# A hand-written order for every engine up to the last weight conversion, with two token blocks sharing layer 1's first pass

## The chip, the cores and the metric

One core of a Trainium2 chip runs the whole program. Its engines are named as the profile names them: PE multiplies matrices (PEld loads its weights), DVE and ACT work on vectors, POOL does little here, and SP and ACT issue DMAs. The metric is the device time of one execution in microseconds (us); the median of three runs before the change is 971.0 us (968.24 to 971.59).

## What is computed

A linear attention with decay over 4 batches, 8 heads, 768 positions and a head size of 48, and behind it two feed-forward layers on 3072 tokens of 384 features with 2048 hidden features each:

```python
for t in range(S):
    state = alpha[:, :, t, :, None] * state + np.einsum('bhd,bhe->bhde', k[:, :, t], v[:, :, t])
    y[:, :, t] = np.einsum('bhd,bhde->bhe', q[:, :, t], state)
...
h = x @ w_in;  g = np.maximum(0.01 * h, h);                   x = g @ w_out     # layer 1
h = x @ w_in;  g = np.where(h > 0, h, np.exp(min(h, 0)) - 1);  x = g @ w_out    # layer 2
```

The weights arrive as 64-bit floats and are converted on the chip.

## The kernel before

**Attention** goes in 24 units of 128 positions (6 units make one batch; the state passes from a unit to the next within it). A unit's chain: `attn_prep` on DVE (a scan E from behind, pe, kS = k times E, a reciprocal, a scan F, qh = q times F); `attn_S` on PE (the scores `sc`, and a transpose `pk` of kS); `attn_S_post` (the mask A on DVE, a copy `kn` of pk on ACT, T on DVE); `attn_V` on PE (`po`, the unit's output, and `pu`, the state's update); `attn_V_post` (xh on ACT and xl on DVE, a two-part split of po, and the state S on DVE). The PSUM pool `ps_a` has three buffers for sc, pk, po and pu together. Four units make a **block** of 512 tokens; behind its last unit `gather` moves rows of x with six DMAs on SP, and only then can the block's first matrix product start.

**Layer 1** goes block by block, 16 steps m each. A step is `ffn1_h` (9 matmuls into hp), `ffn1_g` (t on ACT, max on DVE, gh on ACT, gl on DVE), and `ffn1_y` (9 matmuls that add up in three PSUM tiles y over the 16 steps). h runs two steps ahead of y (`LA = 2`). **Layer 2** does the same with other functions on six blocks.

**The weights of step m** (`both`, m = 0 to 15) are loaded by `stage1` with five DMAs on SP into one of four buffers (x2t0 to x2t3) and converted by `convert_p` (two ACT instructions), `convert_a` (three on DVE, L234, L235 and L237, and the high half on ACT, L238) and `convert_b` (the low half on DVE, L241). Block 0's step m needs conversion m; the other blocks need none.

**What sets the order.** The kernel is traced in one order, and the Tile scheduler then places instructions by its own forecast of when their operands are ready; only the first instruction of convert_p and of convert_a is pinned to program order. So attention, conversions and steps are interleaved by the scheduler. The main program (L574 to L670) runs units 0 to 3 with conversions between them, then block 0's steps with the conversions and with the pieces of units 4 to 7 among them, then the other blocks.

Of the kernel before, what the change touches and what calls it, by code (L numbers as in the profile page):

```python
# [8 lines left out]
F32 = mybir.dt.float32  # L9
# [10 lines left out]
def attention_two_layers_kernel(  # L20
# [79 lines left out]
    vts = {}  # L100
# [21 lines left out]
    def attn_prep(u):  # L122
# [3 lines left out]
        F = at_p.tile([PR, EXT], F32, tag="F", name="F")  # L126
# [5 lines left out]
        nc.vector.tensor_tensor_scan(F[:, 0:EXT - 1], t[:, 0:EXT - 1], d1[:, 0:EXT - 1], 0.0, ALU.mult, ALU.add)  # L132
        e2 = E[:, 1:EXT].rearrange("p (g c) -> p g c", c=C + 1)
        nc.vector.tensor_mul(kS, kS, e2[:, :, 1:C + 1])
        nc.vector.tensor_mul(qh, qh, ext(F, 0)[:, :, 1:C + 1])
        st[u] = dict(kS=kS, qh=qh, pe=pe)

    def attn_S(u):
        c = u % NC
        d = st[u]  # L140
        kS, qh = d["kS"], d["qh"]
        A = at_p.tile([128, 2, NP, C], F32, tag="A", name="A")
# [5 lines left out]
        d["A"], d["sc"] = A, sc  # L148
        if c < NC - 1:
            pk = ps_a.tile([128, NP, PR], F32, tag="at", name="pk")  # L150
            for p in range(NP):
                nc.tensor.transpose(pk[:, p, :], kS[:, p, :], ident[:PR, :PR])
            d["pk"] = pk

    def attn_S_post(u):
        c = u % NC
        d = st[u]
        for j, sc in enumerate(d.pop("sc")):
            nc.vector.tensor_mul(d["A"][:, j], sc, causal.unsqueeze(1).to_broadcast([128, NP, C]))
        if c < NC - 1:  # L160
# [3 lines left out]
        if c > 0:  # L164
# [3 lines left out]

    def attn_V(u):
        c = u % NC  # L170
        d = st[u]
        vt = vts.pop(u)
# [13 lines left out]
        d["po"] = po  # L186
        if c < NC - 1:
# [9 lines left out]
    def attn_V_post(u, xh, xl, off):  # L197
        c = u % NC
        d = st.pop(u)
        po = d["po"]  # L200
        nc.scalar.copy(xh[0:PR, :, off:off + C], po)
        nc.vector.tensor_sub(xl[0:PR, :, off:off + C], po, xh[0:PR, :, off:off + C].bitcast(F32))
        if c < NC - 1:
            pu = d["pu"]
            Sn = at_p.tile([PR, NP, D], F32, tag="S", name="S")
            if c > 0:
                nc.vector.tensor_add(Sn, pu, d["T"])
            else:
                nc.vector.tensor_copy(Sn, pu)
            st["S"] = Sn  # L210

# [48 lines left out]
    def ffn1_g(j, m):  # L260
        n = xt[j][2]
# [493 lines left out]
```

## Time and profile before

| | |
|---|---|
| Median of 3 runs | 971.0 us (968.24 to 971.59) |
| The profiled execution | 971.32 us, of which the span is 969.6 us |
| PE busy | 929.8 us (96% of the span), 5234 matmuls |
| DVE busy | 529.4 us (55%) |
| ACT busy | 445.8 us (46%) |
| The chain that ended last | PE 79%, DVE 8%, DMA 8%, ACT 2% |
| Last matmul ends | about 960 us; then copies and the last output DMA |

The span is divided into 40 slices on the page; PE's digits run 4679 and then 9 to the end, DVE's are 6 to 9 in the first seven slices (up to about 170 us) and fall to 3 later. A matmul's end is modelled, so a busy PE need not be a PE at its peak: what matmuls cost is read from the distance between starts where they follow each other without a break.

### The profile page before, as it was taken

Reading aid. Unit: us, or ns where it says so; the run is one execution under the profiler, and the core shown is the slowest. Engines: PE = TensorE matmul, PEld = TensorE weight load, DVE = VectorE, ACT = ScalarE, POOL = GpSimd, SP = SyncE. Lnnn points to the kernel's source line nnn. Section 1 sums busy time; section 2 is a strip of 40 time slices with the busy share of each in tenths; the row PEclk is TensorE's granted clock in tenths of the full one; section 3 lists DMA queues with packets and bytes.
Section 4 is the critical chain, followed back from the end, with each engine's and each line's share of the span. In section 5 each row is a group of like instructions: output and inputs, shape, how many; then the busy total and the mean of one; then the engine's idle time right before and its main releaser. Section 6 shows DMA issues by size and latency. Waiting matters only on the chain.

```text
span 969.6 us, 13094 instructions
## 1 busy us (share of the span) xinstructions
PE 929.8 (96%) x5234; PEld 781.8 (81%) x5234; DVE 529.4 (55%) x876; ACT 445.8 (46%) x783; POOL 1.1 (0%) x8
## 2 busy tenths in 40 slices
PE   4679999999999999999999999999999999999996
PEld 3557667887888788788878889999999999999995
DVE  6788998534555557454469983433433333333332
ACT  1344545322322323233367795574664744744442
POOL 0000000000000000000000000000000000000000
PEclk9969999999999999999999999999999999999998
DMA  9655561102111221211234330020100200100001
GB/s 243 184 152 160 153 181 45 29 13 58 42 41 41 58 71 53 58 41 50 58 96 141 115 98 10 1 81 1 62 20 1 72 10 1 62 0 1 33 1 37
DMA packets 25093, 62.38 MB, mean 64 GB/s; under 512 B 3936, under 2 KB 7008, under 8 KB 25024
## 3 DMA queue, kind: packets, MB, share of 16 engines
q1 hardware_dynamic: 19184, 40.54, 15.1%
q10 hardware_dynamic: 5840, 20.92, 7.5%
q8 instruction: 43, 0.70, 0.3%
q14 instruction: 26, 0.21, 0.1%
HBM read 54.37 MB, written 4.72 MB: 61 GB/s over the span
## 4 chain that ended last, share of the span: by engine, by line
PE 79%; DVE 8%; DMA 8%; ACT 2%; issue 1%; SPq 1%; DVEq 0%; ACTq 0%
PE hp L310 20%; PE hp L256 16%; PE y L281 15%; PE o L341 10%; PE oa L341 10%; DMA x2t<-in_w_dram 3%; DMA pack<-in_seqs_dram 2%; PE po L178 2%; DMA stg<-in_w_dram 2%; PE sc L147 2%; PE po L184 2%; DMA x<-x 1%; DVE x2t L235 1%; DVE t L265 1%; DVE gl L81 1%
## 5 line engine op out<-in xcount | busy, mean ns | idle before, releaser
L256 PE MATMUL hp<-x,w 128*128 128x512 f32 x864 | 218.6, 395 | 4.1 <-DMA x<-x 2.7
L310 PE MATMUL hp<-x,w 128*128 128x512 f32 x864 | 215.4, 393 | 0.0
L81 DVE TENSOR_TENSOR gl<-t,gh 128x512 fp32r<-128x512 f32 x192 | 132.7, 691 | 126.3 <-ACT gh L78 122.4
L78 ACT CAST gh<-t 128x512 fp32r<-128x512 f32 x192 | 119.0, 620 | 174.1 <-PE y L281 63.9
L256 PEld LDWEIGHTS hp<-x,w 128*128 128x128 f32 x864 | 160.4, 188 | 41.2 <-issue 3.2
L310 PEld LDWEIGHTS hp<-x,w 128*128 128x128 f32 x864 | 160.7, 188 | 29.3
L281 PE MATMUL y<-gh,w 128*128 128x512 f32 x576 | 173.2, 397 | 1.6 <-ACT gh L78 1.6
L319 DVE SCALAR_TENSOR_TENSOR t<-t,hp 128x512 f32<-128x512 f32 x96 | 66.0, 687 | 148.8 <-ACT t L318 148.8
L281 PEld LDWEIGHTS y<-gh,w 128*128 128x128 f32 x576 | 105.5, 188 | 25.6 <-ACT gh L78 3.0
L265 DVE TENSOR_TENSOR t<-t,hp 128x512 f32<-128x512 f32 x96 | 65.4, 683 | 73.8 <-ACT t L264 73.7
L281 PE MATMUL y<-gl,w 128*128 128x512 f32 x288 | 105.3, 394 | 0.0
L317 ACT ACTIVATE t<-hp 128x512 f32<-128x512 f32 x96 | 57.1, 595 | 103.7 <-PE hp L310 103.6
L264 ACT ACTIVATE t<-hp 128x512 f32<-128x512 f32 x96 | 56.8, 594 | 99.2 <-PE hp L256 99.2
L341 PE MATMUL oa<-w,gh 128*128 128x384 f32 x384 | 96.7, 337 | 0.0
L341 PE MATMUL o<-w,gh 128*128 128x384 f32 x384 | 94.7, 337 | 0.2 <-ACT x2t L292 0.2
L341 PEld LDWEIGHTS o<-w,gh 128*128 128x128 f32 x384 | 70.5, 188 | 6.0 <-ACT x2t L292 0.5
L341 PEld LDWEIGHTS oa<-w,gh 128*128 128x128 f32 x384 | 70.2, 188 | 2.9
L281 PEld LDWEIGHTS y<-gl,w 128*128 128x128 f32 x288 | 53.5, 188 | 12.1 <-issue 0.7
L341 PE MATMUL oa<-w,gl 128*128 128x384 f32 x192 | 63.0, 337 | 0.0
L318 ACT ACTIVATE t<-t 128x512 f32<-128x512 f32 x96 | 60.8, 633 | 2.3
L341 PE MATMUL o<-w,gl 128*128 128x384 f32 x192 | 61.0, 336 | 0.0
L147 PEld LDWEIGHTS sc<-pack 48*128 48x128 f32 x384 | 32.0, 210 | 20.3 <-issue 9.3
(89 smaller groups left out, 761.5 us busy)
## 6 DMA issues: line engine op xcount, KB each, us to landing
pack<-in_seqs_dram ACTq DMA_DIRECT2D x21, 674.2 KB, 4.8
stg<-in_w_dram SPq DMA_DIRECT2D x28, 384.0 KB, 3.4
x2t<-in_w_dram SPq DMA_DIRECT2D x20, 384.0 KB, 4.3
vt<-in_vals_dram ACTq DMA_DIRECT2D x21, 288.0 KB, 3.0
span<-in_seqs_dram SPq DMA_DIRECT2D x24, 226.2 KB, 2.7
x2t<-in_w_dram SPq DMA_DIRECT2D x32, 144.0 KB, 3.6
out_dram<-osb SPq DMA_DIRECT2D x24, 192.0 KB, 2.1
x<-x SPq DMA_DIRECT2D x36, 64.0 KB, 4.4
```

The costliest lines, as they stand in the source:

```text
L78: nc.scalar.copy(dst, src)
L81: (lo_engine or nc.vector).tensor_sub(lo, src, dst.bitcast(F32))
L147: nc.tensor.matmul(sc[j][:, p], lhsT=kS[r, p, :], rhs=qh[r, p, :], start=True, stop=True)
L256: nc.tensor.matmul(hp, lhsT=a[:, kk, :], rhs=x[:, kk, :n], start=(i == 0), stop=(i == 3 * KD - 1))
L264: nc.scalar.activation(t, hp, ACTF.Copy, scale=0.01)
L265: nc.vector.tensor_max(t, t, hp)
L281: nc.tensor.matmul(ytiles[j][c], lhsT=a[:, c * 128:(c + 1) * 128], rhs=x, start=(m == 0 and i == 0), stop=(m == KF - 1 and i == 2),)
L310: nc.tensor.matmul(hp, lhsT=a[:, kk, :], rhs=x[:, kk, :], start=(i == 0), stop=(i == 3 * KD - 1))
L317: nc.scalar.activation(t, hp, ACTF.Relu, scale=-1.0)
L318: nc.scalar.activation(t, t, ACTF.Exp, scale=-1.0)
L319: nc.vector.scalar_tensor_tensor(out=t, in0=t, scalar=-1.0, in1=hp, op0=ALU.add, op1=ALU.max)
L341: nc.tensor.matmul(otiles[j][i], lhsT=a[:, i * 128:(i + 1) * 128], rhs=x, start=(m == 0 and n == 0), stop=(m == KF - 1 and n == 2),)
```

## The change

Every instruction up to the step at which the sixteenth conversion is done is chained to the one traced before it on its engine (`in_order`), so on each engine the order is that of the program text; what is traced later is left to the scheduler, and `behind` puts the fallback program behind it. The attention functions are split into their parts (L122 to L257 of the new file), and `quarter(u, i)` runs parts of unit u and of unit u + 1 in a fixed order. Block 0 and block 1 run steps 0 to 3 each, then block 0 its steps 4 to 15, then block 1; y is stored in x2t after the first four steps and added to on DVE at the end. Units 4 to 7 run inside steps 0 and 1, none during the fifteen steps after that (s = 2 to 16), in which the conversions go on at three in four steps; from step 17 on the later units are spread as before. Loads of units 1 and 2 stand ahead of the weights on SP, and from conversion 4 on two weight buffers (x2t2, x2t3) alternate, since x2t0 and x2t1 hold y.

```diff
-        load_v(0)
         load_unit(1)
+        load_v(0)
+        load_unit(2)
+        load_v(1)
         stage1(0)
-        load_v(1)
-        stage1(1)
-        load_unit(2)
         load_v(2)
-        stage1(2)
-        stage1(3)
+        for m in range(1, 4):
+            stage1(m)
...
+        def quarter(u, i, chain=True):
...
+            if i == 0:
+                attn_pu(u)
+                prep_k(u + 1)
+                attn_T(u)
+            elif i == 1:
+                attn_mask(u)
+                if chain:
+                    attn_pk(u + 1)
+                    attn_kn(u + 1)
+                attn_po(u)
+            elif i == 2:
+                prep_F(u + 1)
+                attn_state(u)
+                prep_q(u + 1)
+                if chain:
+                    attn_sc(u + 1)
+                attn_xh(u, xh, off)
+                next_load(u + 3)
+            else:
+                attn_xl(u, xh, xl, off)
+                st.pop(u)
+                if u == blocks[j][0] + blocks[j][1] - 1:
+                    gather(t, blocks[j][1] * C)
...
+        for u in range(UB):
+            for i in range(3):
+                quarter(u, i)
+            if u > 1:
+                conv1.a(u - 1)
+            quarter(u, 3)
+            if u > 1:
+                conv1.b(u - 1)
+            if u > 0:
+                conv1.p(u)
...
+        head, tail = range(FIRST), range(FIRST, KF)
+        seq = [(1, j, m) for ms in (head, tail) for j in range(2) for m in ms]
...
+            if s <= KF:
+                c = 4 if s == 0 else 1 + FIRST + s - 2 - (s - 2) // 4 if s > 1 and s % 4 != 1 else 0
+                ffn1_y(j, m)
+                pe_h(n)
+                ffn1_t(n[1], n[2])
+                conv1.a(c)
+                if s < 2:
+                    for p in quarters[7 * s:7 * s + 7]:
+                        quarter(*p, chain=p[0] + 1 < UB + blocks[1][1])
+                ffn1_max(n[1], n[2])
+                ffn1_gh(n[1], n[2])
+                conv1.b(c)
+                ffn1_gl(n[1], n[2])
+                if c:
+                    conv1.p(c + 1)
+                in_order()
+                continue
```

Three places show how instructions move. The rows of an order name an engine's instructions as the profile does, but for the scans E and F, which stand as SCALAR_TENSOR_TENSOR.

DVE at units 1 and 2, before:

```order
L128 SCALAR_TENSOR_TENSOR E<-pack,d_96 112x517
L130 TENSOR_SCALAR pe<-E 112x4
L134 TENSOR_TENSOR pack<-pack,E 112x512
L202 TENSOR_TENSOR x<-po,x 112x4x128
L131 RECIPROCAL d_97<-pe 112x4
L159 TENSOR_TENSOR A<-sc_252,causal 128x512
L132 SCALAR_TENSOR_TENSOR F<-pack,d_97 112x516
L135 TENSOR_TENSOR pack<-pack,F 112x512
L128 SCALAR_TENSOR_TENSOR E<-pack,d_96 112x517
L159 TENSOR_TENSOR A<-sc_253,causal 128x512
```

and now:

```order
L240 TENSOR_TENSOR x<-po,x 112x4x128
L127 SCALAR_TENSOR_TENSOR E<-pack,d_96 112x517
L129 TENSOR_SCALAR pe<-E 112x4
L130 RECIPROCAL d_97<-pe 112x4
L132 TENSOR_TENSOR pack<-pack,E 112x512
L187 TENSOR_TENSOR T<-S,pe 112x192
L180 TENSOR_TENSOR A<-sc_252,causal 128x512
L180 TENSOR_TENSOR A<-sc_253,causal 128x512
L139 SCALAR_TENSOR_TENSOR F<-pack,d_97 112x516
L248 TENSOR_TENSOR S<-pu,T 112x192
L144 TENSOR_TENSOR pack<-pack,F 112x512
L240 TENSOR_TENSOR x<-po,x 112x4x128
```

The scan E of unit 3 no longer stands between the two halves of unit 1's mask A; each unit's xl (written to x) is followed by the first half of the preparation of the unit after next, and every unit has the same sequence.

DVE at the conversions, before (conversions 7 and 8 among units 5 to 7):

```order
L237 ISA x2t_138<-x2t_134,x2t_138 128x1536
L131 RECIPROCAL d_97<-pe 112x4
L81 TENSOR_TENSOR gl<-t,gh 128x512
L128 SCALAR_TENSOR_TENSOR E<-pack,d_96 112x517
L202 TENSOR_TENSOR x<-po,x 112x4x128
L209 COPY S<-pu 112x192
L241 TENSOR_TENSOR w_7_117<-x2t_139,w_7_116 128x768
L132 SCALAR_TENSOR_TENSOR F<-pack,d_97 112x516
L130 TENSOR_SCALAR pe<-E 112x4
L134 TENSOR_TENSOR pack<-pack,E 112x512
L241 TENSOR_TENSOR w_8_119<-x2t_138,w_8_118 128x768
```

and now (conversions 4 and 5, steps s = 2 and 3):

```order
L275 TENSOR_SCALAR x2t_138<-x2t_136 128x768
L276 SCALAR_TENSOR_TENSOR x2t_138<-x2t_138 128x768
L278 ISA x2t_138<-x2t_136,x2t_138 128x1536
L308 TENSOR_TENSOR t<-t,hp 128x512
L282 TENSOR_TENSOR w_4_111<-x2t_138,w_4_110 128x768
L318 TENSOR_TENSOR gl<-t,gh 128x512
L275 TENSOR_SCALAR x2t_139<-x2t_137 128x768
L276 SCALAR_TENSOR_TENSOR x2t_139<-x2t_139 128x768
L278 ISA x2t_139<-x2t_137,x2t_139 128x1536
L308 TENSOR_TENSOR t<-t,hp 128x512
L282 TENSOR_TENSOR w_5_113<-x2t_139,w_5_112 128x768
L318 TENSOR_TENSOR gl<-t,gh 128x512
```

There is no attention among the conversions any more: a step with a conversion is six instructions on DVE in a fixed order, and a step without one is two.

SP at the start, before:

```order
L107 DMA pack<-in_seqs_dram 112x517
L109 DMA pack<-in_seqs_dram 112x512
L116 DMA vt<-in_vals_dram 128x576
L111 DMA pack<-in_seqs_dram 112x1541
L411 DMA x2t_134<-in_w_dram 48x768
L412 DMA x2t_134<-in_w_dram 16x768
L411 DMA x2t_134<-in_w_dram 48x768
L412 DMA x2t_134<-in_w_dram 16x768
L413 DMA x2t_134<-in_w_dram 128x768
```

and now:

```order
L107 DMA pack<-in_seqs_dram 112x517
L109 DMA pack<-in_seqs_dram 112x512
L111 DMA pack<-in_seqs_dram 112x1541
L116 DMA vt<-in_vals_dram 128x576
L111 DMA pack<-in_seqs_dram 112x1541
L116 DMA vt<-in_vals_dram 128x576
L473 DMA x2t_134<-in_w_dram 48x768
```

The pack of unit 2, which stood behind two steps' weights, is now third, ahead of all weights.

## Rows read from the trace of the kernel before

**Rows 1.** Busy time by engine in three stretches: length, PE, PEld, DVE, ACT, POOL, granted PE clock, DMA.
```profile
0.00:61.00 61.00, 34.59 (x278) 27.84 (x278) 46.24 (x78) 17.29 (x23) 1.08 (x8) 0.88 0.75 199
61.00:164.00 103.00, 99.64 (x644) 73.11 (x646) 94.61 (x148) 49.16 (x73) 0.00 (x0) 0.97 0.51 142
164.00:960.00 796.00, 794.96 (x4316) 680.48 (x4313) 387.55 (x649) 378.46 (x685) 0.00 (x0) 1.00 0.15 44
```

**Rows 2.** The same for PE's L256 (h) and then L281 (y) alone.
```profile
61.00:164.00 103.00, 38.63 (x138) 0.97 0.51 142
...
61.00:164.00 103.00, 34.74 (x126) 0.97 0.51 142
```

**Rows 3.** The chain of waits where PE never stops: start, length, what.
```profile
217.81 2.04 PE hp L256 x9
219.84 1.09 PE sc L147 x16
220.94 2.27 PE y L281 x9
```

**Rows 4.** PE's timeline, same stretch: a unit's two po groups at full speed.
```profile
229.25 1.09 PE L178 MATMUL po<-A,vt 128*64 128x128 f32 x16
230.27 1.08 PE L184 MATMUL po<-pack,T 48*48 48x128 f32 x16
```

**Rows 5.** PE's timeline, first units: the same groups early on.
```profile
26.83 1.94 PE L178 MATMUL po<-A,vt 128*48 128x128 f32 x14 [1.57 <-DVE A L159]
...
30.58 2.08 PE L147 MATMUL sc<-pack 48*128 48x128 f32 x16
35.48 0.98 PE L152 MATMUL pk<-ident,pack 112*128 112x112 f32 x4 [2.82 <-DVE x L202]
42.71 1.19 PE L147 MATMUL sc<-pack 48*128 48x128 f32 x16
```

**Rows 6.** Busy time by engine in a short stretch; columns as in Rows 1.
```profile
54.00:56.00 2.00, 2.00 (x18) 1.77 (x16) 2.00 (x4) 0.91 (x2) 0.00 (x0) 0.50 0.50 149
```

**Rows 7.** DVE's timeline: one preparation, one mask, one xl, one convert_a.
```profile
4.71 1.23 DVE L128 TENSOR_TENSOR_SCAN E<-pack,d 112x517 f32<-112x517 f32 x1 [2.64 <-DMA pack<-in_seqs_dram]
6.86 1.23 DVE L132 TENSOR_TENSOR_SCAN F<-pack,d 112x516 f32<-112x516 f32 x1
...
13.86 1.28 DVE L159 TENSOR_TENSOR A<-sc,causal 128x512 f32<-128x512 f32 x2
...
55.56 0.69 DVE L202 TENSOR_TENSOR x<-po,x 112x512 fp32r<-112x512 f32 x1
...
87.05 0.56 DVE L234 TENSOR_SCALAR x2t<-x2t 128x768 int32<-128x768 int32 x1
...
88.71 0.96 DVE L237 CUSTOM_DVE_ANT_0 x2t<-x2t,x2t 128x1536 uint16<-128x1536 uint16 x1
```

**Rows 8.** ACT's groups up to 250 us: count, busy us, mean ns, idle time before.
```profile
L78 ACT CAST gh<-t 128x512 fp32r<-128x512 f32 x34 | 21.1, 621 | 39.2 <-DVE t L265 20.7 <-PE y L281 18.4
...
L230 ACT ACTIVATE x2t<-x2t 128x768 int32<-128x768 uint16 x16 | 14.6, 913 | 40.5 <-DMA x2t<-in_w_dram 39.0 <-PE po L178 1.5
L238 ACT CAST w<-x2t 128x768 fp32r<-128x768 f32 x16 | 13.3, 830 | 13.9 <-DVE x2t L237 13.9
L201 ACT CAST x<-po 112x512 fp32r<-112x512 f32 x12 | 6.9, 582 | 3.3 <-PE po L184 3.3
```

**Rows 9.** What DVE waited for up to 110 us: us in total, times, longest.
```profile
DVE E L128 <- DMA pack<-in_seqs_dram: 12.6, 8, 2.7
```

**Rows 10.** PE's timeline: block 0's first h.
```profile
61.19 1.19 PE L256 MATMUL hp<-x,w 128*128 128x512 f32 x2 [1.88 <-DMA x<-x]
```

**Rows 11.** Line L413, the last of a step's five weight loads: us to landing.
```profile
DMA to landing us min/median/max: 3.3/4.3/5.8
```

**Rows 12.** Timelines of ACT and of SP's queue: one issue of a DMA each.
```profile
30.95 0.35 ACTq L116 DMA_DIRECT2D vt<-in_vals_dram  x1
...
73.26 0.42 SPq L413 DMA_DIRECT2D x2t<-in_w_dram  x1
```

More of the change, by code (lines that the diff above doesn't have):

```diff
@@ L163, in attn_S_post, with attn_mask, attn_T @@
             d["kn"] = kn
-        if c > 0:
+    def attn_mask(u):
+        d = st[u]
+        A = at_p.tile([128, 2, NP, C], F32, tag="A", name="A")
+        for j, sc in enumerate(d.pop("sc")):
+            nc.vector.tensor_mul(A[:, j], sc, causal.unsqueeze(1).to_broadcast([128, NP, C]))
+        d["A"] = A
+    def attn_T(u):
+        d = st[u]
+        if u % NC > 0:
             T = at_p.tile([PR, NP, D], F32, tag="cT", name="T")
@@ L186, in attn_V, with attn_pu @@
         d["po"] = po
+    def attn_pu(u):
+        c = u % NC
+        d = st[u]
+        vt = vts[u]
         if c < NC - 1:
@@ L275, in ffn1_y @@
         gh, gl = steps.pop((1, j, m))
-        if m == 0:
+        first, last = parts(j, m)
+        if first:
             ytiles[j] = [ps_y.tile([128, n], F32, tag=f"y{c}", name=f"y{c}") for c in range(KD)]
@@ L282, in ffn1_y @@
                     ytiles[j][c], lhsT=a[:, c * 128:(c + 1) * 128], rhs=x,
-                    start=(m == 0 and i == 0), stop=(m == KF - 1 and i == 2),
+                    start=(first and i == 0), stop=(last and i == 2),
                 )
-        if m == KF - 1:
+        if last:
             t0 = blocks[j][0] * C
@@ L475, in b @@
                 self.done[2] += 1
-                if self.layer == 1 and m + 4 < KF:
-                    stage1(m + 4)
+                if self.layer == 1 and m >= 2 and m + 2 < KF:
+                    stage1(m + 2)
     spans = {}
@@ L572, in general, with in_order, behind @@
                 ffn2_y(j, m)
+    traced = [0]
+    def in_order():
+        ins = list(nc.cur_bb.bb.instructions)
+        last = {}
+        for i, x in enumerate(ins):
+            y = last.get(x.engine)
+            if i >= traced[0] and y is not None:
+                tc.add_manual_dep(
+                    x, y.name,
+                    mybir.DependencyInfo(mybir.DependencyClass.NoSync, mybir.DependencyReason.DATA),
+                    reason="in_order")
+            last[x.engine] = x
+        traced[0] = len(ins)
+    def behind():
+        ins = list(nc.cur_bb.bb.instructions)
+        last = {x.engine: x for x in ins[:traced[0]]}
+        for x in ins[traced[0]:]:
+            if x.engine in last:
+                tc.add_manual_dep(
+                    x, last[x.engine].name,
+                    mybir.DependencyInfo(mybir.DependencyClass.NoSync, mybir.DependencyReason.DATA),
+                    reason="behind")
     with ExitStack():
@@ L590, in attention_two_layers_kernel @@
         LA = 2
[L592 to L608 removed]
+        UB = blocks[0][1]
@@ L609, in attention_two_layers_kernel @@
+        ffn1_max(0, 0)
+        ffn1_gh(0, 0)
+        quarter(UB, 2)
+        ffn1_h(0, 1)
+        ffn1_t(0, 1)
+        ffn1_gl(0, 0)
+        conv1.p(UB)
+        ffn1_max(0, 1)
+        ffn1_gh(0, 1)
+        ffn1_gl(0, 1)
+        in_order()
+        head, tail = range(FIRST), range(FIRST, KF)
+        seq = [(1, j, m) for ms in (head, tail) for j in range(2) for m in ms]
+        seq += [(1, j, m) for j in range(2, NB) for m in range(KF)]
         seq += [(2, j, m) for j in range(NT // 512) for m in range(KF)]
@@ L668, in attention_two_layers_kernel @@
                     guard()
+        behind()
         with tc.If(nc.values_load(near, min_val=0, max_val=1) == 0):
```

163 lines of the change are left out of this document (95 added, 68 removed).

## The prediction

> **What bounds the kernel now.** I read busy time by stretch first. From 164 us on PE is busy 794.96 of 796 us [rows 1], and the last 9.6 us of the span are copies and output; nothing the change does to DVE, ACT or the queues can shorten that part unless PE has less left to do. Ahead of 164 us it is different: DVE is busy 94.6 of the 103 us from 61 on and PE's matmuls are spread out. So the question is how far the work has come when PE stops waiting.
>
> At full speed nine matmuls of a step take 2.04 us, 0.227 each. An attention unit takes 1.09 for sc [rows 3] and 1.02 for each half of po (start to start) [rows 4]; pk and pu are taken at 0.5 each, half of pk's 0.98 at half speed [rows 5]. That is 4.1 us in 68 matmuls, 0.06 each. Up to 164 us PE had 278 + 644 = 922 matmuls [rows 1], 264 of them for layer 1 [rows 2]: 264 x 0.227 + 658 x 0.06 = 99.4 us of work in 164 us. About 65 us are lost there, and the change can move only those.
>
> **How I add up.** Let T be the start of block 1's first h in the new order, from where on PE should hardly stop. By then it has done four h and three y (63 matmuls) and eight units (492 attention matmuls). To come to where the old order stood at 164 us it needs 201 x 0.227 = 45.6 us and 166 x 0.06 = 10.0 us, and 2.3 us for about ten attention groups between steps, each of which makes the group behind it 0.23 us longer (2.27 against 2.04) [rows 3]. With 3 us of stalls (below) that is T + 60.9.
>
> **T, first part: units 0 to 3.** The scan of unit 0 starts at 4.71 as before, and the old chain then waits for packs, 12.6 us in eight waits [rows 9]. Now the packs of units 1 and 2 are ahead of the weights on SP, and unit 3's, issued by ACT, has until about 27 us; I count no wait for packs. If that cover is gone, unit 3 costs up to the 2.7 us of the longest wait. E to F is 2.15 us, a mask A 1.28 [rows 7]; q, of xl's size, is taken like xl's 0.69, which makes a preparation 4.1. Unit 0's scores end at 11.0. Its pk, kn, pu and unit 1's pk then stand ahead of its po (three groups of about 1.0 and a copy of 0.6), so po starts at 14.6, xl ends at 17.9, and unit 1's mask starts at 20.3.
>
> From there the chain of one unit is: half of A 0.7, then pk 1.0 (its PSUM buffer is the one that this half of A frees), po 3.85 (twice 1.94 [rows 5], the second starting a little earlier), xh 0.6 [rows 8], xl 0.7, the next unit's E to kS 2.15 [rows 7], T 0.3 (192 columns against xl's 512): 9.3 us at PE's half speed. F, S and q lie beside po. So unit 2's mask starts at 29.6. With a conversion in it the unit is 1.7 longer: convert_a (2.6, from 87.05 to the end of 88.71) [rows 7] fits beside po, but the high half waits on ACT behind two DMA issues of 0.35 [rows 12] (0.83 us itself [rows 8]), and the low half, taken at 0.9 by L237's 0.96, stands ahead of the next scan. Unit 3's mask starts at 40.6, its xl at 46.9, ending at 47.5. From xl's end to block 0's first h it was 61.19 - 56.25 = 4.9 us for the gather [rows 7, 10]; now h starts at 52.4, 8.8 us earlier than before.
>
> **T, second part: steps 0 to 3 and units 4 to 7.** From 47.5 on DVE does, in its order and counted from start to start (taken as some 0.1 us less than the durations of rows 7): four E to kS (8.6), four A (4.8), four F and q (7.1), S and T three times each (1.6), four xl (2.4), two convert_a (5.2), three low halves (2.6), three max and three gl at 0.6, as gh (3.6): 35.9 us. In-order waits come on top: max(0,0) for h 1.4, max(0,1) for h(0,1) 3.4 (it stands behind po(4) and sc(5) on PE), gl(0,1) 1.7 (its gh stands behind 1.8 us of convert_p on ACT) [rows 8], xl(5) 3.1 for po at half speed, xl(6) 2.4 (its xh stands behind the step's t, and that behind y(0,1) and h(0,3)), xl(7) 0.8: 12.8 us. Unit 7's xl ends at 96.3, with 4.9 for the gather h(1,0) starts at 101.2; y(0,2) alone can cover the gather, so PE idles some 4 us. If po(7) runs at half speed too, it is 103.
>
> **PE's speed** decides how much of this is paid. [...] In the new order PE has some 8 us (pk, po, pu and the next sc by the rows at half speed) in a unit's 9.3, so a part should run at full speed: I take 2.5 us off, T = 100.5, nearer to the half-speed end since most rows are there. All at full speed T is 94, all at half speed 112 (rivals).
>
> [...]
>
> **Stalls after T.** A step with a conversion has on ACT t 0.6 (of gh's size), the high half 0.83, gh 0.62 and the next convert_p, two at 0.91 [rows 8], 3.9 us, and the loop from gh through convert_p, convert_a, the high half and back to gh is about 4.35 us by these and rows 7; one step in four has no conversion, so four steps take about 17.0 against PE's 16.3. Block changes add three copies to ACT twice. With h two steps ahead there are about 2 us of slack. I count 3 us of stalls until the last conversion; bounds 0 and 14 (the loads, below). The adds of y on DVE, three per block, lie beside PE's next h; after step 16 DVE has room, as in 164 to 960 (387.6 of 796 us) [rows 1].
>
> **Sum.** 100.5 + 60.9 = 161.4 us for what took 164: 2.6 us less. The profiled execution had 971.32 us for a span of 969.6, and its time is 0.3 above the median; 971.0 - 2.6 gives **968.4 us**. About 0.5% (4.9 us) is what a measurement of this kernel can tell from no change, so this forecast lies within it.
>
> **Rivals.**
> *PE comes to full speed early.* For it: in the new order PE's runs in a unit are longer, and at 42.71 full speed did come. Against it: the run at 54 us stayed slow. It saves 2.2 on unit 1's period, 1.5 around units 2 and 3, where DVE's 2.6 us of conversion then is the longer side, 1.3 at the first h, 2.0 at xl(5) and 2.0 at po(7), 9 us from 103: T = 94, 6.5 less than the forecast: 962 us.
> *PE stays at half speed through the second part.* One mechanism, at 60 to 105 us: the gaps keep the clock low while DVE is waiting for matmuls. From 103 us, h(0,1) and sc(5) cost 3 more on the chain, y(0,1) with h(0,3) 4.1, the first h of block 1 and what follows 2: T = 112, 11.5 more: 980 us. It decides if the granted clock is 0.5 through most of that stretch. For it: rows 6. Against it: the whole stretch from 61 to 164 us has a clock of 0.97 in the old order, though PE's work is as broken up there [rows 1].
> *The weight loads become the bound.* With two buffers the load for step m + 2 starts when convert_a of step m ends, and convert_p wants it 5.7 us later. The last of five issues, 0.42 each [rows 12] and a short gap between them, starts 1.9 us after the first and lands after 3.3 to 5.8, median 4.3 [rows 11]: 6.2 at the median, within the 3 us counted, but 7.7 at the longest, 2 us late in eight of twelve loads, 16 us less 2 of slack, 11 above the 3 counted: 979 us. Against it: no packs are loaded in that stretch now.
> That the order does not take hold is no rival: the rows of the order show it.
>
> **How the numbers follow.** Forecast 0.46 (964.9 to 972), full speed 0.30, half speed 0.13, loads 0.11. Faster by over 0.5% (below 966.1): 0.28 of the second and 0.10 from the forecast's lower edge, 0.38. Slower by over 0.5% (above 975.9): 0.11 + 0.09 of the two slow rivals and 0.02 of the forecast, 0.22. The rest, 0.40, is within 0.5%. The range 960 to 978 holds the forecast, nearly all of the second and half of each slow rival, leaving out less than 2 in 10; the forecast's own range is 965 to 972.
>
> **What would show it.** Block 0's first h at about 52 us and block 1's at about 100; no DVE wait for packs over 1 us; DVE waiting some 13 us for xh and t between 47 and 97; the last low half at about 162; PE idle under 3 us from block 1's first h on. A sc group of 1.1 us before 40 us speaks for full speed; a clock of 0.5 from 60 to 100 or PE waits for gh after 105 us, with ACT waiting for weights, make the forecast wrong.

## The result and the profile after

| | before | changed |
|---|---|---|
| Median | 970.4 us (968.24 to 971.59, 4 runs) | 980.4 us (979.94 to 983.39, 4 runs) |
| Ratio to before | | 1.011, 95% interval 1.0086 to 1.0134 |
| Span of the profiled execution | 969.6 us | 978.2 us |
| Block 0's first h starts | 61.19 | 54.77 |
| Block 1's first h starts | about 166.5 (the group of 15 at 165.09 begins with the last six of block 0's) | 109.11 |

The change makes the kernel slower by about 1.1%, 10 us. The forecast was 968.4 with a range of 960 to 978, so the time lies 2.4 us outside it, on the side of the rival "PE stays at half speed through the second part" (980).

Busy time by engine of the changed kernel, the stretches and columns of [rows 1]:

```profile
0.00:61.00 61.00, 36.59 (x315) 29.29 (x317) 44.10 (x76) 14.29 (x20) 1.15 (x8) 0.72 0.68 185
61.00:164.00 103.00, 84.80 (x458) 65.31 (x455) 72.63 (x106) 48.53 (x74) 0.00 (x0) 0.90 0.42 117
```

and of PE's h (L297) and y (L341) alone, as [rows 2]:

```profile
61.00:164.00 103.00, 35.10 (x135) 26.31 (x135) 0.90 0.42 117
...
61.00:164.00 103.00, 36.78 (x133) 26.16 (x134) 0.90 0.42 117
```

PE starts 37 matmuls more in the first 61 us (315 against 278), then far fewer: 458 against 644 in the 103 us after it, though four more of them are of layer 1 (268 against 264). DVE is busy 72.6 of these 103 us where it was 94.6. And PE's granted clock, 0.97 in that stretch before, is 0.90; in the first stretch it fell from 0.88 to 0.72.

Where the early gain goes is read from the same view with windows that begin at 0, by the working of the prediction: 0.227 us for each matmul of h and y, 0.06 for each of attention, and what the clock on the wall shows beyond that is lost. Some records are missing (PE x315 and PEld x317 in the first row above), so half a microsecond means nothing here.

| up to | before: matmuls (of layer 1) | lost, us | changed: matmuls (of layer 1) | lost, us |
|---|---|---|---|---|
| 47 us | 210 (0) | 34.4 | 262 (0) | 31.3 |
| 70 us | 334 (16) | 47.3 | 374 (34) | 41.9 |
| 90 us | 451 (81) | 49.4 | 477 (49) | 53.2 |
| 109 us | 572 (132) | 52.6 | 555 (63) | 65.2 |
| 164 us | 922 (264) | 64.6 | 769 (277) | 71.6 |

At 70 us the new order is 5.4 us ahead. From there to 109 us it loses 23 us in 39, the old one 5. After that it loses less than the old one (6.4 against 12.0), but not enough. So it is the stretch in which units 4 to 7 run inside two steps.

The chain of waits of the changed kernel (start, length, what) goes through both gathers and through a stretch in which PE has nothing that it may start (the profile calls it issue; pk(6), at 75.31, stands behind DVE's kS of unit 6, which runs from 74.55 to 75.21):

```profile
0.81 3.68 DMA pack<-in_seqs_dram
8.75 2.08 PE sc L158 x16
19.87 8.43 DMA pack<-in_seqs_dram
50.33 5.25 DMA x<-x
...
70.68 4.63 issue
76.30 2.38 PE po L212 x16
...
102.77 6.20 DMA x<-x
109.11 4.10 PE hp L297 x9
```

PE's timeline in that stretch shows the gaps, and the speed behind each:

```profile
55.72 3.94 PE L297 MATMUL hp<-x,w 128*128 128x512 f32 x8 [0.19 <-DMA x<-x]
...
68.46 2.20 PE L297 MATMUL hp<-x,w 128*128 128x512 f32 x9
75.31 0.98 PE L166 MATMUL pk<-ident,pack 112*128 112x112 f32 x4 [4.65 <-issue]
76.23 2.45 PE L212 MATMUL po<-A,vt 128*64 128x128 f32 x16
...
83.84 0.61 PE L166 MATMUL pk<-ident,pack 112*128 112x112 f32 x4 [2.07 <-DVE A L180]
84.44 1.09 PE L212 MATMUL po<-A,vt 128*64 128x128 f32 x16
85.45 1.22 PE L341 MATMUL y<-gh,w 128*128 128x512 f32 x2
...
96.33 2.54 PE L212 MATMUL po<-A,vt 128*64 128x128 f32 x16 [2.34 <-DVE A L180]
98.80 1.95 PE L218 MATMUL po<-pack,T 48*48 48x128 f32 x16
...
109.11 4.09 PE L297 MATMUL hp<-x,w 128*128 128x512 f32 x9 [5.25 <-DMA x<-x]
```

Nine matmuls of h take 2.20 by duration at 68.46 and 4.09 at 109.11; po takes 1.09 at 84.44, and 2.45 and 2.54 behind the gaps of 4.65 and 2.34 us. What DVE waited for in the first 110 us has changed its place too, against [rows 9]:

```profile
DVE x L240 <- ACT x L237: 13.8, 7, 4.1
DVE t L308 <- ACT t L303: 7.2, 2, 3.6
DVE E L127 <- DMA pack<-in_seqs_dram: 4.5, 2, 2.4
```

The packs cost 4.5 instead of 12.6 us, and DVE now waits for xh, which waits for po, and for the first t, which waits for h.

### The profile page after: what moved, and what is told of

Same layout as the page of the kernel before. It is cut to its first block, busy times and chain, and to the rows that moved or that the text cites. A ratio compares the mean times of both kernels' runs of the same rounds, so it can differ in the third digit from the quotient of the medians.

```text
span 978.2 us, 13129 instructions
## 1 busy us (share of the span) xinstructions
PE 925.1 (95%) x5234; PEld 781.3 (80%) x5234; DVE 535.3 (55%) x880; ACT 446.2 (46%) x785; POOL 1.1 (0%) x8
## 4 chain that ended last, share of the span: by engine, by line
PE 83%; DVE 7%; ACT 4%; DMA 3%; issue 1%; SPq 0%; ACTq 0%; DVEq 0%
PE hp L372 20%; PE y L341 17%; PE hp L297 17%; PE oa L403 10%; PE o L403 10%; PE po L212 3%; PE sc L158 2%; PE po L218 2%; DMA pack<-in_seqs_dram 2%; DVE x2t L278 1%; DMA x<-x 1%; DVE E L127 1%; DVE x2t L276 1%; PE pk L166 1%; ACT x2t L270 1%
## 5 line engine op out<-in xcount | busy, mean ns | idle before, releaser
L297 PE MATMUL hp<-x,w 128*128 128x512 f32 x864 | 218.6, 396 | 11.2 <-DMA x<-x 10.3
L297 PEld LDWEIGHTS hp<-x,w 128*128 128x128 f32 x864 | 163.3, 190 | 49.1 <-issue 10.8
L341 PE MATMUL y<-gh,w 128*128 128x512 f32 x576 | 179.4, 400 | 2.0 <-ACT x2t L354 1.0
L341 PEld LDWEIGHTS y<-gh,w 128*128 128x128 f32 x576 | 106.6, 190 | 26.5 <-ACT x2t L354 2.0
L341 PE MATMUL y<-gl,w 128*128 128x512 f32 x288 | 109.8, 396 | 1.0 <-DVE gl L318 0.9
L308 DVE TENSOR_TENSOR t<-t,hp 128x512 f32<-128x512 f32 x96 | 65.4, 681 | 71.6 <-ACT t L303 71.5
L403 PE MATMUL o<-w,gh 128*128 128x384 f32 x384 | 94.6, 336 | 0.0
L341 PEld LDWEIGHTS y<-gl,w 128*128 128x128 f32 x288 | 54.5, 190 | 14.6 <-DVE gl L318 2.7
```

What stands on the lines that cost most here:

```text
L297: nc.tensor.matmul(hp, lhsT=a[:, kk, :], rhs=x[:, kk, :n], start=(i == 0), stop=(i == 3 * KD - 1))
L308: nc.vector.tensor_max(t, t, hp)
L341: nc.tensor.matmul(ytiles[j][c], lhsT=a[:, c * 128:(c + 1) * 128], rhs=x, start=(first and i == 0), stop=(last and i == 2),)
L403: nc.tensor.matmul(otiles[j][i], lhsT=a[:, i * 128:(i + 1) * 128], rhs=x, start=(m == 0 and n == 0), stop=(m == KF - 1 and n == 2),)
```

## Experiments

Two theories stood first. **CLOCK**: the gaps bring PE to half speed, and the groups behind them are on the units' chain. **CHAIN**: the chain itself over DVE, PE and ACT has too little other work beside it, whatever PE's speed. A third, **ORDER**, is that a fixed order costs waits wherever it is. Times of all runs, each with three rounds (e17 and e18 five), beside runs of the kernel before on the same chip (median 971.1 for e1 to e4, 973.0 for e5 to e8, 970.2 for e9 to e12, 970.8 for e13 to e16, 971.5 for e17 and e18):

| run | median, us | ratio to before, 95% interval | h(0,0), h(1,0) start at |
|---|---|---|---|
| the change | 980.4 | 1.0110 (1.0086 to 1.0134) | 54.8, 109.1 |
| e1 gaps filled | 973.9 | 1.0039 (1.0018 to 1.0059) | 54.5, 101.5 |
| e2 six shared steps | 978.9 | 1.0083 (1.0058 to 1.0107) | 54.5, 112.0 |
| e3 no sharing | 972.0 | 1.0005 (0.9984 to 1.0027) | 54.3, 157.1 |
| e4 no chains | 984.3 | 1.0132 (1.0102 to 1.0163) | 66.8, 125.0 |
| e5 gather on two queues | 981.0 | 1.0077 (1.0050 to 1.0103) | 55.3, 111.3 |
| e6 old order of loads | 981.1 | 1.0082 (1.0055 to 1.0110) | 56.9, 113.2 |
| e7 = e1, convert_p early | 983.1 | 1.0098 (1.0069 to 1.0128) | 54.2, 102.2 |
| e8 = e3, low half on POOL | 982.8 | 1.0106 (1.0075 to 1.0137) | 54.5, 170.3 |
| e9 two gaps filled | 978.6 | 1.0074 (1.0055 to 1.0094) | 54.1, 110.3 |
| e10 = e2, filled | 974.6 | 1.0044 (1.0027 to 1.0061) | 55.2, 111.6 |
| e11 eight shared steps | 979.9 | 1.0091 (1.0074 to 1.0108) | 54.2, 130.1 |
| e12 = e11, two gaps filled | 977.5 | 1.0070 (1.0051 to 1.0089) | 54.7, 126.7 |
| e13 = e1, filled from the start | 973.8 | 1.0034 (1.0021 to 1.0048) | 53.6, 103.1 |
| e14 = e10, two in three conversions | 972.8 | 1.0031 (1.0015 to 1.0048) | 54.4, 110.2 |
| e15 = e14, filled from the start | 972.4 | 1.0028 (1.0005 to 1.0051) | 51.8, 108.6 |
| e16 = e3, filled from the start | 969.5 | 0.9988 (0.9969 to 1.0008) | 51.0, 153.2 |
| e17 = e16, pack 3 ahead of weights | 966.1 | 0.9955 (0.9937 to 0.9973) | 50.8, 154.4 |
| e18 = e15, pack 3 ahead of weights | 966.2 | 0.9953 (0.9934 to 0.9971) | 48.9, 105.9 |

The starts are those of each profiled execution. h(1,0) comes with six steps of block 0 done in e2, e10, e14, e15 and e18, eight in e11 and e12, sixteen in e3, e8, e16 and e17 and four in the others, and is to be compared only within these.

**e1: PE's gaps filled.** `zero` is a tile of zeros; `fill(k)` is `warm` into block 0's y and adds nothing, a `warm` into hp is overwritten by h.

```diff
+    def warm(dst, rhs, k, start):
+        for i in range(k):
+            nc.tensor.matmul(dst, lhsT=zero, rhs=rhs, start=start, stop=start, skip_group_check=True)
...
+        if (j, m) == (0, 0):
+            warm(hp[:, 0:384], both[0][0][:, 0:384], 16, True)
+        if (j, m) == (1, 0):
+            warm(hp, xt[0][0][:, 0, :], 22, True)
...
                 attn_mask(u)
+                if u in (5, 6, 7):
+                    fill({5: 19, 6: 8, 7: 8}[u])
```

> The changed kernel with matmuls that add nothing put into TensorE's idle stretches between 50 and 109 us: 16 ahead of block 0's first h, 19 ahead of pk(6), 8 ahead of pk(7), 8 ahead of po(7), 22 ahead of block 1's first h (the zero weights add 0 to y, or are overwritten in hp). Theory CLOCK (the groups behind each gap run at half speed, and that is what put block 1's first h 9 us late): the half-speed groups h(0,0), po(4), pk(6), po(6), y(0,1), po(7), y(0,2), h(1,0) cost about 12 us, most of it on the chain; block 1's first h moves from 109 to about 101 and the time from 980.4 to 971 to 974. Theory CHAIN (the units' chain over DVE, ACT and PE has too little other PE work beside it, whatever the speed): PE is as late as DVE lets it, block 1's first h at 106 or later, time 977 to 982.

Busy time from 47 to 105 us, of the change:

```profile
47.00:105.00 58.00, 41.07 (x295) 31.23 (x295) 38.82 (x63) 15.83 (x24) 0.00 (x0) 0.76 0.44 117
```

and of e1:

```profile
47.00:105.00 58.00, 50.96 (x384) 39.50 (x381) 40.81 (x64) 16.16 (x25) 0.00 (x0) 1.00 0.53 140
```

PE's timeline of e1 behind the same gaps:

```profile
68.33 4.47 PE L335 MATMUL y<-x,zero 128*128 128x512 f32 x19
73.14 0.57 PE L167 MATMUL pk<-ident,pack 112*128 112x112 f32 x4 [0.35 <-issue]
...
93.31 1.08 PE L219 MATMUL po<-pack,T 48*48 48x128 f32 x16
...
96.51 5.15 PE L335 MATMUL hp<-x,zero 128*128 128x512 f32 x22
101.50 0.39 PE L302 MATMUL hp<-x,w 128*128 128x512 f32 x1
```

The granted clock is 1.00 through the stretch instead of 0.76, pk and po are at full speed, block 1's first h comes 7.6 us earlier, and the time falls by 6.5 us. 73 matmuls that compute nothing make the kernel faster, with the intervals apart, and what they change in the profile is PE's speed. (The po behind pk(6) is unit 5's, and that behind pk(7) unit 6's; the expectation calls the first po(6).) CLOCK is shown. It is not all: with h(1,0) at 101.5, about where the forecast had it, the kernel is still 0.39% slower than before.

**e2, e11: more shared steps.** `FIRST` from 4 to 6 (or 8), the quarters over 4 (6) steps, and the conversions that the two (four) more steps need among them.

```diff
-    FIRST = 4
+    FIRST = 6
...
-                    for p in quarters[7 * s:7 * s + 7]:
+                    for p in quarters[[0, 4, 7, 10, 13][s]:[4, 7, 10, 13][s]]:
```

> The changed kernel with blocks 0 and 1 taking six steps each instead of four before block 0 goes on, the quarters of units 4 to 7 spread over four steps (4, 3, 3, 3) instead of two (7, 6), and conversions 4 and 5 among them. Theory CHAIN: the two more steps (8.2 us of PE work) fall into the gaps, and DVE's waits from 47 us on (19 us) shrink by about half; block 1's first h comes at 110 to 114, but with two steps more done: time 972 to 976. Theory ORDER (a fixed order on each engine makes every engine wait for the slowest instruction ahead, however the units are spread): no gain, 979 to 985. Theory CLOCK: smaller gaps, so a gain as well, 974 to 978.

> Eight shared steps each; the quarters of units 4 to 7 over six steps (3, 2, 2, 2, 2, 2) with conversions 4 to 8 among them, and the other eight conversions one in two steps behind. Theory COVER: 24 us of h and y stand beside the units, DVE (about 50 us of work in these six steps) becomes the bound; block 1's first h at 113 to 118 with eight steps done, and no stalls behind it, where a step comes in 4.1 to 4.2 us: 968 to 973. Theory ORDER (a fixed order costs waits however it is spread): 976 to 982.

e2 is 0.3% below the change by its ratio, with overlapping intervals and less than CHAIN wanted, and e11, where it wanted most, no better: block 1's first h comes at 130.1, not at 113 to 118. More cover alone does not help. A likely reason, not tested: more steps beside the units bring more conversions, and these stand ahead of the units' instructions on DVE.

**e3: hand order, no sharing.** `FIRST = 16`, one quarter in each of steps 0 to 13, one conversion in each of steps 0 to 12, four weight buffers.

> The hand-made order kept, but blocks not shared: block 0 runs its 16 steps, then block 1 its 16; one quarter of units 4 to 7 in each of steps 0 to 13 and one conversion in each of steps 0 to 12; y is not stored in between, four weight buffers. Theory CHAIN: the early gain (block 0's first h at 54.8 instead of 61.2) is kept and the crammed units are gone; DVE bounds the 13 steps at some 6 us each, PE is dense from about 140 us on: 964 to 970, faster than the kernel before. Theory ORDER: the in-order waits stay, 976 to 985.

It is as fast as the kernel before (1.0005): the sharing, with the crammed units and the two weight buffers that go with it, costs the 1%, not the fixed order. But the 6 us won at 54 us do not arrive either. Busy time from 70 to 140 us of e3:

```profile
70.00:140.00 70.00, 57.72 (x329) 43.63 (x329) 65.39 (x94) 41.08 (x59) 0.00 (x0) 0.94 0.47 130
```

DVE is busy 65.4 of 70 us there, PE 57.7. That fits DVE as the bound; e8 was to show it.

**e4: no chains.** `in_order` adds no dependencies; the text is the same.

> The changed kernel without the chains that pin each engine's order: the program text, with the sharing and the crammed units, is the same, and the scheduler places instructions. Theory ORDER: the scheduler fills the waits, 968 to 974. Theory CHAIN: the text gives the scheduler no other PE work to put into the gaps before block 1's first h but block 0's next steps, whose weights are not converted: 977 to 984.

984.3 us, and block 0's first h at 66.8 instead of 54.8. ORDER falls: the fixed order is what brings the first h forward, and without it the same text is no faster (the intervals overlap).

**e5: gather on two queues.**

```diff
-            nc.sync.dma_start(
+            (nc.scalar if b % 2 else nc.sync).dma_start(
                 x[hi:hi + 16, :, b // 2, :n].bitcast(F32), x[lo:lo + 16, :, KD, :n].bitcast(F32))
```

> The changed kernel with a block's six gather DMAs issued alternately by SP and ACT instead of all by SP. From xl's end to the block's first h it took 6.5 and 7.0 us, where 4.9 were counted, and six issues on one queue take 3.9 of them. Theory ISSUE: three issues take half, block 0's first h comes 1.5 to 2 us earlier, block 1's 3 to 4 in all: 976 to 978. Theory LANDING (the transfers themselves, behind weight loads, set the time): no gain, 979 to 982.

The six issues are done in 2.3 us instead of 3.9, yet h follows xl by 6.8 and 6.6 us, as in the change (6.5 and 7.0); neither h comes earlier (55.3 and 111.3), and the interval overlaps that of the change. The issues are not what the gather costs.

**e6: the old order of loads.**

> The changed kernel with the loads on SP in the order of the kernel before (unit 2's pack behind two steps' weights). Theory LOADS (the early gain, about 5 us at 61 us, comes from the packs standing ahead of the weights): the scans of units 1 and 2 wait 3 to 5 us each, every mark after it moves by 4 to 8 us, and as nothing hides it the time is 984 to 988. Theory ORDER (the gain comes from the order of the units' own instructions): packs land in time or nearly so, 980 to 982.

981.1 us, the same as the change within the intervals, where LOADS wanted 984 us and more. In its profile, which is of its slowest execution (985.0), the first h comes 2.1 us later, and 4.1 at block 1. Most of the early gain comes from the order of the units' instructions, not from the packs of units 1 and 2.

**e7: convert_p earlier,** on top of e1.

```diff
+                if s > 1 and c:
+                    conv1.p(c + 1)
                 conv1.a(c)
```

> The kernel with the idle stretches filled (e1_warm) and the next conversion's two ACT instructions put ahead of convert_a instead of behind the step's gl, from step 2 on. After block 1's first h a step took 4.5 us, not 4.08. Theory LOOP (gh, then convert_p, convert_a, the high half, then gh again follow one another): the steps come down to 4.1 to 4.2 us and the time from 973.9 to 968 to 971. Theory DVE (six instructions, 4.6 us in a step with a conversion): little gain, 972 to 975.

Both theories fall: 983.1 us, 9 slower than e1. What ACT waited for between 105 and 172 us in e7:

```profile
ACT x2t L271 <- DMA x2t<-in_w_dram: 11.1, 4, 3.4
```

convert_p now stands ahead of its weights' landing, and t and gh behind it wait with it. So with two buffers the load is the next bound, close behind.

**e8: low halves on POOL,** on top of e3.

```diff
-        nc.vector.tensor_sub(lo, ts.bitcast(F32), hi.bitcast(F32))
+        (nc.gpsimd if nconv[0] <= KF else nc.vector).tensor_sub(lo, ts.bitcast(F32), hi.bitcast(F32))
```

> The hand order without shared blocks (e3_no_share) with the low half of every layer-1 conversion on POOL instead of DVE, which takes 0.87 us each off DVE. Theory DVE (DVE is the bound between 70 and 140 us there, so the 6 us gained early cannot reach the end): thirteen low halves off DVE give 6 to 11 us, 961 to 966. Theory LATENCY (the order's waits bound it): 970 to 974. If POOL is much slower at it than DVE and h waits for its low half, 975 and more.

POOL's group from 50 to 170 us:

```profile
L282 POOL TENSOR_TENSOR w<-x2t,w 128x768 fp32r<-128x768 f32 x15 | 27.4, 1829 | 98.6 <-ACT w L279 98.6
```

1.83 us on POOL against 0.96 on DVE, and PE's h waits 6.8 us for it from 50 to 170 (6.0 for DVE's in e3): 982.8 us. Nor does DVE win what it hands over. Some of its own instructions that meet a subtraction on POOL take far longer:

```profile
79.02 1.82 POOL L282 TENSOR_TENSOR w<-x2t,w 128x768 fp32r<-128x768 f32 x1 [4.12 <-ACT w L279]
79.26 1.61 DVE L129 TENSOR_SCALAR pe<-E 112x4 f32<-112x4 f32 x1
```

From 50 to 170 us pe takes 1612 ns in the mean instead of e3's 171, and gl 1060 instead of 688. So e8 says nothing about DVE as the bound; that stays open.

**e9: only the two gaps in front of a first h filled.**

> The changed kernel with only the two gaps in front of a block's first h filled (16 and 22 added matmuls that are overwritten), none ahead of pk(6), pk(7), po(7). Theory CLOCK, every gap costs its share: the groups at half speed right behind these two gaps cost 2.7 + 0.9 us (h(0,0), po(4)) and 1.9 (h(1,0)); the other three gaps keep theirs (pk and po behind them), so about half of e1_warm's 6.5 us: 975 to 978. Rival: one early fill is enough, since a fast start makes the later gaps shorter: 972 to 975. Rival: the two gaps are covered by the gather anyway: 979 to 982.

978.6 us, 0.2% below the change in time and 0.4% by its ratio, with overlapping intervals, between what CLOCK and the rival of the covered gaps wanted, and h(1,0) at 110.3. The 2 us that the fast first h wins are lost again at po(5), sc(6), po(6) and po(7), which run at half speed (2.54, 2.08, 1.97 and 2.54 us). Here the clock had to be held through the chain (e1: 1.00 from 47 to 105 us, 973.9 us), not only at its ends.

**e10, e12: longer heads, filled.**

> Six shared steps each (e2_first6) with the idle stretches filled (16, 19, 4, 4 and 22 added matmuls). Theory COVER + CLOCK (the two add up, since the one gives PE other work and the other its speed): 978.9 less the 5 to 7 us that filling gave with four steps: 971 to 974, and PE stands at 164 us as the kernel before or better. Theory SAME LOSS (both act on the same idle time): 976 to 979.

> Eight shared steps (e11) with the two gaps in front of a block's first h filled (16 and 22 added matmuls). Theory CLOCK: the first h at full speed and what follows it, 3 to 5 us less than e11: 964 to 969, which would be faster than the kernel before. Theory DVE (DVE is the bound in that stretch, PE's speed does not matter): within 1.5 us of e11.

e10 gains 4.2 us on e2, less than the 5 to 7 that COVER + CLOCK wanted and with intervals that just touch, and is not faster than e1. e12 gains 2.4 on e11, within the two intervals. In e12's PE timeline, behind h(1,0), the h groups of steps with a conversion every second time:

```profile
152.02 2.20 PE L302 MATMUL hp<-x,w 128*128 128x512 f32 x9
156.10 2.20 PE L302 MATMUL hp<-x,w 128*128 128x512 f32 x9
```

They start 4.08 us apart, PE's own pace, seven times in a row from 135.70 to 164.26. In the change, with three conversions in four steps:

```profile
150.40 2.20 PE L297 MATMUL hp<-x,w 128*128 128x512 f32 x9
...
154.48 2.20 PE L297 MATMUL hp<-x,w 128*128 128x512 f32 x9
...
159.43 2.20 PE L297 MATMUL hp<-x,w 128*128 128x512 f32 x9
...
164.52 2.20 PE L297 MATMUL hp<-x,w 128*128 128x512 f32 x9
```

4.08, 4.95 and 5.09 apart; over the twelve steps from 115.07 to 169.23 us it is 4.51.

**e13 to e16: filled from the start, and the rhythm.** Ahead of sc(0), pk(2), pk(3) and pk(4) stand 12, 8, 14 and 10 products of the identity with itself (`yz` is read by nobody); e14 spreads e10's last ten conversions over steps 4 to 18.

```diff
+        yz = ps_y.tile([128, 512], F32, tag="y0", name="yz")
+        def fill0(k):
+            for i in range(k):
+                nc.tensor.matmul(yz[:, 0:128], lhsT=ident, rhs=ident, start=True, stop=True, skip_group_check=True)
```

> e1_warm (four shared steps, five filled stretches) with four more filled: 12, 8, 14 and 10 added 128x128 matmuls ahead of sc(0), pk(2), pk(3) and pk(4), written to a tile that nothing reads. Theory CLOCK from the start: pk and po of units 0 to 3 go from half to full speed, 1 us less for pk and po's two halves each on a chain of 10.6 us per unit, so that block 0's first h comes 3 to 6 us earlier and the time is 968 to 971. Theory DVE/LOADS: in the first 47 us a unit's period is set by DVE (prep, mask, conversion) and by the packs, PE's speed is hidden: 973 to 975.

> e10 (six shared steps, filled) with the last ten conversions spread over steps 4 to 18, two in three, instead of three in four. Eight shared steps with a conversion every second step ran at 4.08 us a step, the changed kernel at 4.5. Theory RHYTHM (the loop of conversion, weight load and gh bounds three in four, not two in three): 2 to 3 us less than e10, 971 to 973. Rival: the stalls only move: 974 to 976.

> e14 with the four early fills of e13 as well. If CLOCK holds from the start and RHYTHM holds, the gains add up: 966 to 969, faster than the kernel before. If the early speed is hidden: 971 to 973.

> The hand order without shared blocks (e3, 972.0 us) with the four early fills and the one ahead of block 0's first h. Theory DVE (DVE is the bound from 70 to 140 us there, busy 17 to 19 of each 20 us): what is won ahead of 55 us is kept, since DVE starts the conversions that much earlier: 966 to 970. Theory CLOCK elsewhere or none: the fills win nothing at the end, 971 to 973.

None of the steps e1 to e13, e10 to e14, e14 to e15 can be told apart by its intervals. e13's first h comes 0.8 us earlier than e1's, not 3 to 6. What took the early gain is one row of DVE's timeline, the scan of unit 3:

```profile
29.12 1.23 DVE L128 TENSOR_TENSOR_SCAN E<-pack,d 112x517 f32<-112x517 f32 x1 [4.30 <-DMA pack<-in_seqs_dram]
```

The wait for that pack, 2.11 us in the change, is 4.30 here: DVE comes earlier, the pack does not. ACT issues it at 19.87 us in the change and at 22.02 here, behind the weights of four steps on SP. e16 is not to be told from the kernel before.

**e17, e18: unit 3's pack ahead of the weights of steps 2 and 3,** and issued by SP instead of ACT.

```diff
+            eng = nc.sync if u == 3 else nc.scalar
+            load_unit(u, eng=eng)
+            load_v(u, eng=eng)
+            if u == 3:
+                stage1(2)
+                stage1(3)
...
-        for m in range(1, 4):
-            stage1(m)
+        stage1(1)
```

> e16 (hand order, no shared blocks, filled early stretches; 969.5 us, not to be told from the kernel before) with unit 3's pack and values issued by SP ahead of the weights of steps 2 and 3 instead of by ACT behind them. In the kernels filled from the start DVE waited 4.3 us for that pack, and TensorE's speed was eaten there. Theory PACK: that wait goes, block 0's first h comes 2 to 4 us earlier, and DVE, the bound until 140 us, keeps it: 965 to 968, faster than the kernel before. Theory DVE IDLE ELSEWHERE (weights come later instead, a conversion waits): 969 to 972.

> e15 (six shared steps, everything filled, 972.4 us) with unit 3's pack and values issued by SP ahead of the weights of steps 2 and 3. Theory PACK: 2 to 4 us earlier at block 0's first h and kept, since PE is what is late there: 968 to 970.5. Rival: the wait comes back at the next gather or pack: 972 to 974.

The same scan in e18:

```profile
24.80 1.23 DVE L128 TENSOR_TENSOR_SCAN E<-pack,d 112x517 f32<-112x517 f32 x1
```

No wait, 2.9 us earlier than in e15 (27.69), block 0's first h 2.9 and block 1's 2.7 us earlier, and the time 972.4 to 966.2, ratio 1.0028 to 0.9953, intervals apart. The marks carry about half of these 6.2 us: PE's last matmul ends 2.8 us earlier (958.35 against 961.14), and what else came is not in them. Both e17 and e18 are faster than the kernel before by about 0.45%, 5 us; e17 and e16 cannot be told apart by their intervals. In e17's profiled execution, the slowest of its six, the wait is gone as well, but its first h comes at 50.79 against e16's 50.98: there the fills ahead of pk(2) ran at half speed,

```profile
19.56 3.46 PE L732 MATMUL yz<-ident 128*128 128x128 f32 x16
```

where they took 2.05 us in e16. So the profiles show the pack's part in e18; for e17 they do not.

## Why the prediction was wrong

**The first part of T held.** Unit masks were forecast at 20.3, 29.6 and 40.6 us and came at 20.0, 30.7 and 41.4; xl(3) was to end at 47.5 and ended at 48.2. "I count no wait for packs" was wrong by 2.1 us at unit 3, inside the 2.7 that were named as its cost.

**The gathers were mis-sized.** 4.9 us were counted from xl's end to the first h, from [rows 7, 10]; they took 6.5 and 7.0 (48.24 to 54.77, 102.10 to 109.11), 3.7 us more in both, the largest single term of the miss. The six issues took no longer than before (3.93 against 4.04 us); the way from issue to landing did, here for the gather before and for blocks 0 and 1 now:

```profile
DMA to landing us min/median/max: 2.4/3.0/4.2
...
DMA to landing us min/median/max: 4.6/5.4/6.0
...
DMA to landing us min/median/max: 4.7/5.6/6.4
```

In the new order ACT issues a later unit's pack (674 KB) and values (288 KB) 1.3 and 0.9 us ahead of each gather (six times 64 KB):

```profile
46.99 0.32 ACTq L111 DMA_DIRECT2D pack<-in_seqs_dram  x1
47.40 0.39 ACTq L116 DMA_DIRECT2D vt<-in_vals_dram  x1
...
48.27 3.93 SPq L262 DMA_DIRECT2D x<-x  x6
```

In the kernel before, such a pack was issued 2.5 us ahead of the gather (54.11 and 56.58). In e15 and e18 it is issued 3.0 us ahead of block 0's gather, the median landing is 2.4 and 2.9 us, and h follows xl by 5.1; ahead of block 1's, where it is 1.3 us again, the median is 4.3 and 4.5. So the sum, it seems, left out what else moves beside the gather. This is read from the traces; no run moves that pack alone.

**The second part of T is where the mechanism failed.** From block 0's first h to xl(7)'s end 43.9 us were counted (52.4 to 96.3), and it took 47.3. The step that failed is "so a part should run at full speed: I take 2.5 us off". It went from how much of a unit PE is busy (8 of 9.3 us) to PE's speed; that was the author's estimate, and no run shows that step: from 47 to 105 us the granted clock was 0.76 with PE busy 41.07 of 58 us, 0.83 in the kernel before with 52.71, and 1.00 in e1 with 50.96. A part did run at full speed, but two groups on the chain that the sum of 101.2 has at full speed, y(0,1) and po(7), came at half speed. DVE's waits for xl(6) and xl(7), counted as 2.4 and 0.8 us, were

```profile
92.57 0.69 DVE L240 TENSOR_TENSOR x<-po,x 112x512 fp32r<-112x512 f32 x1 [4.13 <-ACT x L237]
...
101.41 0.69 DVE L240 TENSOR_TENSOR x<-po,x 112x512 fp32r<-112x512 f32 x1 [2.55 <-ACT x L237]
```

and in e1, at full speed, very nearly what was counted:

```profile
87.95 0.69 DVE L241 TENSOR_TENSOR x<-po,x 112x512 fp32r<-112x512 f32 x1 [2.55 <-ACT x L238]
...
95.06 0.69 DVE L241 TENSOR_TENSOR x<-po,x 112x512 fp32r<-112x512 f32 x1 [0.82 <-ACT x L238]
```

These two are 3.5 us longer than counted, xl(5) is 1.3 shorter (1.8 instead of 3.1), and the rest of the 3.4 comes in small pieces. The wait at max(0,0), 3.6 instead of 1.4, is mostly block 0's late gather over again: that first h was counted at half speed. Together: 0.7 (xl(3)) + 3.7 (gathers) + 3.4 + 0.7 (what the 2.5 had left below 101.2) = 8.5 of the 8.6 us by which T missed 100.5.

e1's 7.6 us are not the same sum, since the forecast had much of the chain at half speed already. By its own savings T would be 97.7 with the second part alone at full speed (103 less 1.3, 2.0 and 2.0). e1, at a clock of 1.00 in that part, has 101.5, and that this is near the forecast's 100.5 is luck: gathers too short against groups counted slow.

**The rival had the mechanism.** "PE stays at half speed through the second part" gave T = 112 and 980 us, at a chance of 0.13; T was 109.1, the time 980.4. Its condition, a clock of 0.5 through most of 60 to 105 us, held in part: the mean was 0.76 from 47 to 105. Two of its three places are in the profile as it named them (the first h of block 1 at 4.09, y behind a gap); the third, h(0,1) with sc(5), ran at full speed, and pk(6), po(5) and po(7) were slow in its place. Its argument against itself, the 0.97 of the old order, was no evidence: there PE was busy 99.6 of the 103 us [rows 1], now 84.8. What speaks for this rival is the trace: behind four gaps, of 4.65, 2.34, 2.07 and 5.25 us, come groups at half speed, with 2.45, 2.54, 1.22 (two matmuls of y, behind pk and po at full speed) and 4.09 us. With the gaps filled (e1) the granted clock is 1.00 from 47 to 105 us.

**Stalls behind T.** 3 us were counted, and "one step in four has no conversion, so four steps take about 17.0 against PE's 16.3". Four steps took 18.0 (4 x 4.51); over twelve steps that is 5.2 us above PE's pace. The mechanism was right, the size not. The loop was put at 4.35, but the rows that it names add up to 5.2: gh 0.62, two of convert_p at 0.91, two of convert_a at 0.96, the high half 0.83. ACT's gh in steps with a conversion shows it at 5.09:

```profile
150.88 0.62 ACT L312 CAST gh<-t 128x512 fp32r<-128x512 f32 x1
...
155.97 0.61 ACT L312 CAST gh<-t 128x512 fp32r<-128x512 f32 x1
...
161.06 0.61 ACT L312 CAST gh<-t 128x512 fp32r<-128x512 f32 x1
```

With a conversion every second step the steps come at PE's pace (e12). That the loads would become the bound did not come true at this rhythm, but e7 shows that they stand right behind. 11.2 us of error in the span (967.0 forecast, 978.2 measured) are thus 8.6 at T and 2.6 behind it; in e1, whose span is 973.3, they are 1.0 at T and 5.3 behind it.

**Open.** Whether DVE bounds e3 and e16 (e8 did not tell), what e14's rhythm is worth in time, whether the pack issued ahead of a gather is what slows it, why e17 gains what its profiled execution does not show, and where e18's gain beyond 2.8 us comes from.

## What to carry to other kernels

Where units of work form a chain over several engines, do not pack them together to free a later stretch: PE's gaps between them cost twice here, once as idle time (4.65, 2.34 and 5.25 us) and once as half speed in the groups behind (po 2.45 and 2.54 us instead of 1.09, h 4.09 instead of 2.20), and these groups are on the chain. Where no work was at hand for the gaps, matmuls that compute nothing held the speed here (a granted clock of 1.00 in e1 where the change had 0.76, and 7.6 us at block 1's first h); with only two of five gaps filled nothing was won that could be told (e9). Before counting a gain at an early mark, ask which transfer and which engine will be late next: here it was one pack behind weights that nobody needed yet. With it moved and the gaps filled, both forms of the order were faster than the kernel before (ratios 0.9955 and 0.9953), and for the form with shared steps the move itself is clear of the noise. And when a transfer is on the chain, look at what is issued just ahead of it.

## What was not expected of the hardware

In the change, half speed did not show in every group right behind a gap: behind the 2.07 us ahead of 83.84 pk and po ran at full speed (0.61 and 1.09), and y, 1.6 us later and with PE busy in between, did not (1.22 for two matmuls that took 0.61 at 66.42). In the kernels with the early fills the same fill ran at either speed, 2.05 us in e16 and 3.46 in e17. Matmuls with zero weights, whose products change nothing, held the granted clock at 1.00 in e1 from 47 to 105 us, as real ones did in the kernel before from 164 us on [rows 1]. A subtraction of 128x768 that DVE does in 0.96 us took 1.83 on POOL in e8, and beside it one of DVE's small instructions took 1.61 us instead of 0.17. The gather's transfers of 64 KB took a median of 5.4 us to land in the change, with a bulk load issued 1.3 us ahead of the first, and 3.0 in the kernel before, with one issued 2.5 us ahead.
